# Complex products summed on GpSimd before every second inverse transform step of a long convolution

## The chip, the cores and the metric

The kernel runs on one core of one Trainium2 chip. The metric is the device time of one execution in microseconds. The engines of a core run side by side, each with an instruction queue of its own, and wait for one another through semaphores: TensorE (PE, matmuls, with its weight loads as PEld), VectorE (DVE), ScalarE (ACT), GpSimd (POOL), and SyncE (SP), which issues most of the transfers here.

## The reference

One block of a network with two halves. The first is a gated long convolution (H3), the second an MLP with a matrix over positions (gMLP). Both are modulated by vectors from a condition `c`.

```python
x = A_q                                             # 1 x 2048 x 640, bf16
sa, ca, ga, sb, cb, gb = six rows of silu(c) @ w_mod
h = layernorm(x) * (1 + ca) + sa
# first half
kv  = (causal convolution of A_k with 4 taps) * A_v
y_f = rfft(kv padded to 4096) * rfft(ssm_k padded to 4096)   # per channel, complex
y   = irfft(y_f)[:2048] + kv * ssm_D
x   = x + ga * (h * y)
# second half
h = layernorm(x) * (1 + cb) + sb
z = gelu(h @ w_in)                                  # 640 -> 2 x 864
g = w_sp @ layernorm(z[:, 864:]) + b_sp             # 2048 x 2048 over the positions
x = x + gb * ((z[:, :864] * g) @ w_out)
```

## The kernel before

The transforms are matmuls with tables of cosines and sines that the kernel makes itself. The 640 channels are worked on as five units of 128 (`u`), each in eight steps (`st`) of two frequency blocks (`KP = 2`). For a unit there is a first stage (`s1`) for the kernel's spectrum (K) and one for the signal (U), then the forward steps, the product of the two spectra, and the inverse steps. The results of the eight inverse steps are collected in `Z`; `Z` is transposed by a DMA (PE for the last unit), and a last small matmul (`y` or `yl`) gives `y`, which is multiplied into the modulated input `gh`.

```python
def forward(name, X1, st, extra=()):
    ...
        for k in range(KP):
            kc = st * KP + k
            mm(pu[:, k], M2[:, 0, kc, :], x[:, 2 * kc:2 * kc + 2, :], True, False)      # 256 columns
            mm(pu[:, k, 0], M2[:, 2, kc, :], x[:, 2 * kc + 1, :], False, False)         # 128 columns
            mm(pu[:, k, 1], M2[:, 1, kc, :], x[:, 2 * kc, :], False, True)

def u_item(u, st):
    forward(pu, "X1U%d" % u, st)

    def product(e):                       # real/imaginary of the signal x real/imaginary of the kernel
        T_ = new(T, "T", [P, KP, 2, 2, DU])                                  # bf16
        e.tensor_tensor(T_[:], tl[pu][:, :, :, None, :].to_broadcast([P, KP, 2, 2, DU]),
                        tl[KH][:, :, None, :, :].to_broadcast([P, KP, 2, 2, DU]), op=ALU.mult)
    op("D", "prod", product, r=[pu, KH], w=[T], new=[(T, "T")])

    def inv(e):
        ...
        for k in range(KP):
            kc = st * KP + k
            mm(p_[:, k], G2[:, 0, kc, :], T_[:, k, 0], True, False)          # 256 columns
            mm(p_[:, k], G2[:, 1, kc, :], T_[:, k, 1], False, False)         # 256 columns
            mm(p_[:, k, 1], G2[:, 2, kc, :], T_[:, k, 0, 0], False, False)   # 128 columns each
            mm(p_[:, k, 0], G2[:, 1, kc, :], T_[:, k, 0, 1], False, False)
            mm(p_[:, k, 1], G2[:, 0, kc, :], T_[:, k, 1, 0], False, False)
            mm(p_[:, k, 0], G2[:, 3, kc, :], T_[:, k, 1, 1], False, True)
    op("P", "inv", inv, ...)
    op("AD", "zc", ...)                   # copy of the result from PSUM into Z
```

All four partial products of a complex product are kept, and the matmuls of the inverse step add them up in PSUM.

Other operations that share the time with these:

```python
op("P", "taps", ...); op("D", "tv", ...)           # the short convolution as four matmuls, times v
op("SA", "kvw", ...)                               # kv goes to DRAM and is read back in another order
op("A", "khc", ...)                                # kernel spectrum: PSUM -> KH
op("AD", "s1c", ...)                               # first stage: PSUM -> X1
op("GD", "ghm", ...)                               # modulation of gh: a multiplication and an addition
op("D", "ym", ...)                                 # gh *= y
op("GD", "res", ...); op("D", "ln2", ...)          # residual addition, statistics of the second layernorm
op("P", "zz", ...); op("A", "gelu", ...)           # second half: z products, gelu
op("P", "fill", ...)                               # matmuls into an unused bank; they only keep PE active
```

An operation is registered with the engines on which it may run (`"GD"`: GpSimd or VectorE), what it reads and what it writes. A long list fixes which engine takes which operation and in what order; every engine works through its part of the list strictly in that order.

```python
FILLS = (4, 4, 4, 1, 2, 1, 1, 1, 3, 1, 2, 2, )
SLOTS = dict(X=4, X1=4, KH=9, T=4, Z=3, ZT=1, wm=1, big=2, dg=2, st1=2, s1=1, sm=2, pu=2, pz=2)   # buffers per kind
ORDER = """
D13 D95 D12 D96 S14 D97 D103 D109 D104 D110 A0 D115 A5 A4 A1 A2 A3 A111 D98 A99 D6 D18 P979 P980 P981 P19 S16 A112 P21
... 991 entries: a letter for the engine (P, A, D, G, S) and the number of the operation ...
"""
```

Once all of this has been issued, the mixing over the positions begins (`mix`, `project`): 32 groups of 16 matmuls of 432 columns and 32 of 7 matmuls of 320 columns, with nothing else large beside them.

Of the kernel before, what the change touches and what calls it, by code (L numbers as in the profile page):

```python
# [15 lines left out]
P = 128  # L16
# [9 lines left out]
DU = 128  # L26
# [7 lines left out]
FILLS = (4, 4, 4, 1, 2, 1, 1, 1, 3, 1, 2, 2, )  # L34
SLOTS = dict(X=4, X1=4, KH=9, T=4, Z=3, ZT=1, wm=1, big=2, dg=2, st1=2, s1=1, sm=2, pu=2, pz=2)
# [4 lines left out]
D13 D95 D12 D96 S14 D97 D103 D109 D104 D110 A0 D115 A5 A4 A1 A2 A3 A111 D98 A99 D6 D18 P979 P980 P981 P19 S16 A112 P21  # L40
D7 D8 D9 S77 D81 S78 A10 D11 G124 G125 D20 P139 A106 D82 D141 P142 A105 A140 A144 P982 P145 A146 D22 G31 D143 D116
D121 A100 G101 A118 S15 P983 P25 S17 D26 P148 S467 P23 D24 S27 A117 G107 A150 P127 D128 A149 A147 S29 G102 P984 P151
A152 P153 A154 S28 G113 S30 G119 P133 A120 G108 P157 A158 P985 P163 S79 A164 P165 A166 D471 D472 P130 D134 P155 A156
G114 P159 A131 D473 D474 P36 G43 D135 P161 D37 A160 P38 D39 P986 P167 D168 A162 A169 G129 P170 A172 P34 A171 S80 P176
A177 D178 P173 D175 P32 A174 S83 P179 D35 P187 P136 D85 P211 D180 D33 G132 P181 S468 D188 D182 A212 P191 P215 P189
A216 D192 S41 A190 P203 D204 P217 A218 P193 A194 D137 P195 S40 D196 P207 S42 P213 D208 D138 P46 P183 D184 P50 A475
P199 S84 A476 D477 D47 A214 P205 A206 P197 D200 A198 P235 A236 P221 D478 A222 D51 P44 P239 A240 P219 A220 D479 G480
P209 A210 P237 S470 D486 P223 P231 A238 A232 D45 P48 A224 D487 P241 A242 D49 S509 P510 A511 P512 A513 D488 D481 A493
S86 D88 D497 P243 D244 A498 G67 D494 P229 A230 P275 G55 A276 P201 D202 P225 A226 P185 S469 S52 D482 P263 P279 A280
P245 A186 A246 D264 D495 S514 P251 D252 P267 S87 P277 A278 D499 D268 P265 A266 P255 A122 D256 P281 A282 D500 P515 P247  # L50
D248 A483 D496 P517 D516 D537 P289 A290 D518 P299 A300 A489 P253 D254 S53 S54 P269 G616 D484 D485 G556 D490 G491 P301
A302 P62 P233 A234 D123 P227 D63 D492 A270 A228 P60 P303 P283 A304 P295 A284 D501 D502 D61 A296 P249 G558 P305 A505
S519 P293 D506 P287 A288 D507 A294 P56 A250 D57 S65 D503 P58 D59 D504 P297 A306 S89 P291 D91 P520 D535 A298 G539 P307
A292 D308 D521 G540 P339 A340 A508 G541 G536 P271 P522 D523 P257 D272 G599 P319 D320 P341 A342 P309 A310 D258 P315
D316 P343 A344 P335 D336 P68 P345 S66 D69 P273 A274 G538 D542 P259 G557 D260 P321 S64 P285 A346 D322 D562 S543 P544
D545 G563 P72 D73 A286 G595 P261 A262 P546 P347 A348 D547 P331 D332 D620 S90 P363 A364 P548 D560 P337 A338 P317 A318
G559 D549 P367 P550 D551 G554 A368 P359 A360 P327 D328 D552 G597 P70 P369 P361 A362 G655 G656 P311 P329 A330 P323 D370
D312 D324 P74 D75 D71 P351 A352 D651 S697 P365 A366 P325 A326 P357 A358 S92 D94 P333 A334 S564 D561 P565 D566 G618
G598 P371 D372 S76 S93 P403 A404 P349 A350 P567 D568 G657 D596 P313 P355 P569 A356 G619 P387 D570 G593 A314 P407 G553
A408 D388 P379 D380 P571 D572 P373 A374 P405 A406 P375 D376 P381 G578 D581 P409 A410 P391 A382 P353 D392 A354 D579  # L60
P389 G573 D576 P427 A428 P395 S601 G653 D654 A390 P377 A378 D396 P429 D600 P399 D400 P397 P383 D384 G594 S698 P602
D603 G583 A430 P431 S524 A432 P423 A424 D587 P401 A402 P415 A416 P433 A434 G588 G617 P604 D577 D575 D398 D605 P425
A426 P411 A412 D652 P393 D574 A394 P435 D436 P419 A420 P606 D607 P385 G658 P451 D452 P443 D444 D582 P608 P437 D438
A386 P417 A418 P525 P421 A422 P447 G614 G615 A526 S622 P453 A454 D609 D613 D448 P455 D456 P445 A446 P463 D464 P449
P459 P457 D460 D580 G611 G621 A450 P413 D610 A414 P623 D624 P439 D440 A458 P465 P625 D626 P461 D462 A466 P441 S527
A442 P627 D628 P528 A529 P665 D666 S530 P663 D664 P629 D630 P659 P661 D662 D631 D632 D633 A660 P987 P667 D668 P676
G555 D669 P683 D670 D671 D699 P690 D700 D672 D684 P531 A532 P533 D634 G701 D702 D703 D704 P705 D673 A534 D706 D674
D715 P988 P713 A714 P711 D712 P989 P709 A710 G636 D675 D635 P707 D708 P990 P763 A764 P731 A732 D716 D677 D640 D637
P759 G717 D718 D691 D720 D719 D678 P729 A730 P723 A724 D681 A760 P741 A742 P765 D682 D784 D679 P725 A726 D639 D641
P727 A728 P761 D781 D680 A766 G646 P721 A722 D638 D783 D782 D586 D648 G785 D786 D787 A788 D789 A762 P738 D790 A739  # L70
S791 P734 P767 A768 D685 D686 P773 A774 A735 P745 A746 D688 P752 A753 P755 A756 D687 D736 A792 D743 P748 G612 A794
D642 A749 D740 D744 P769 D584 D643 D847 P771 A772 D793 D795 D796 P825 A826 A770 D585 P839 A840 P797 A798 D644 P837
A838 P807 P814 A808 D692 P827 A828 A815 P833 A834 D689 P829 A830 D696 D849 D757 D592 D645 P835 A836 D848 D850 G851
D695 D852 D853 D855 D856 D854 D809 S857 P804 A805 D694 D733 D590 D914 D589 D647 P800 A801 D754 P831 A832 D693 D913
D650 A858 D816 D859 D860 D861 P811 A812 P821 A822 P818 D862 P866 P887 D649 A819 P863 A888 A864 D916 D591 D915 G917
P870 D806 A871 D918 D919 D920 D922 D921 A867 P877 D813 D817 D868 P899 D758 D872 A900 P905 A878 A906 D747 S923 D925
D924 D750 P880 A881 A927 D928 P873 A874 D875 P901 D802 A902 P903 A904 D810 D926 P884 A885 P929 A930 P946 D820 D823
A947 P932 A933 D876 P893 A894 D882 P939 P950 D751 A940 P959 P957 D737 G775 A951 A958 D879 D883 A960 D799 P897 A898
D934 P943 A944 D803 D824 D776 D889 D777 D886 G841 D842 P953 A845 P936 A937 A954 A780 P963 A964 D948 D846 P895 A896
A843 D778 P969 D890 P971 A972 D865 D869 G907 D908 D911 D909 D910 A970 P891 A892 A779 P967 P965 A966 D912 D955 D952  # L80
D956 D938 D945 D949 D941 D942 D931 D935 G973 A844 D974 A977 D976 D975 A126 P961 A962 A968 D978
# [39 lines left out]
def kernel(  # L121
# [80 lines left out]
    with ExitStack() as actx:  # L202
# [56 lines left out]
        mbase = consta.tile([P, KCH, QH], F32, name="mbase")  # L259
# [4 lines left out]
        nc.gpsimd.iota(pint[:], [[0, 1]], base=0, channel_multiplier=1)  # L264
        nc.gpsimd.iota(f1k[:], [[4, NKC], [0, 2]], base=1, channel_multiplier=0, allow_small_or_imprecise_dtypes=True)
        nc.gpsimd.iota(f1r[:], [[0, NKC], [16, 2]], base=48, channel_multiplier=0, allow_small_or_imprecise_dtypes=True)
        nc.gpsimd.memset(mpi[:], -2.0 * HALF_PI)
        nc.gpsimd.iota(pidx[:], [[0, 1]], base=0, channel_multiplier=1, allow_small_or_imprecise_dtypes=True)
        nc.gpsimd.iota(fidx[:], [[1, P]], base=0, channel_multiplier=0, allow_small_or_imprecise_dtypes=True)
        nc.gpsimd.iota(mbase[:], [[4, KCH], [64, QH]], base=1, channel_multiplier=0, allow_small_or_imprecise_dtypes=True)  # L270
# [44 lines left out]
        def m2_base():  # L315
            def steps(e):
                e.tensor_scalar(mstep[:, 0:NCH], fidx[:, 0:NCH], pidx[:, 0:1], 4.0 * KCH / 8192.0, op0=ALU.mult, op1=ALU.mult)
                e.tensor_scalar(mstep[:, NCH:], mstep[:, 0:NCH], 0.25, None, op0=ALU.add)
                e.tensor_scalar(mturn[:], mstep[:], TWO_PI, None, op0=ALU.mult)
            op("D", "mstep", steps, w=["mstep"])  # L320
            op("D", "mbase", lambda e: e.tensor_scalar(mbase[:], mbase[:], pidx[:, 0:1], 1.0 / 8192.0, op0=ALU.mult, op1=ALU.mult),
               w=["mbase"])

        def m2_chunk(i):
# [4 lines left out]
            def turns(e):  # L329
                new(a, "T", [P, 2, KCH, QH], F32)  # L330
                for h in range(2):
                    e.tensor_scalar(tl[a][:, h], mbase[:], mstep[:, h * NCH + i:h * NCH + i + 1], MAGIC, op0=ALU.add, op1=ALU.add)
            op("DG", "turns", turns, r=["mbase", "mstep"], w=[a], new=[(a, "T")])
            op("D", "msub", lambda e: e.scalar_tensor_tensor(tl[a][:], tl[a][:], MAGIC, mbase[:, None].to_broadcast([P, 2, KCH, QH]),
# [104 lines left out]
        def u_item(u, st):  # L439
# [4 lines left out]

            def product(e):
                T_ = new(T, "T", [P, KP, 2, 2, DU])
                e.tensor_tensor(T_[:], tl[pu][:, :, :, None, :].to_broadcast([P, KP, 2, 2, DU]),  # L447
                                tl[KH][:, :, None, :, :].to_broadcast([P, KP, 2, 2, DU]), op=ALU.mult)
            op("D", "prod", product, r=[pu, KH], w=[T], new=[(T, "T")])

            def inv(e):
# [4 lines left out]
                for k in range(KP):  # L456
                    kc = st * KP + k
                    mm(p_[:, k], G2[:, 0, kc, :], T_[:, k, 0], True, False)
# [527 lines left out]
```

## Time and profile before

| | |
|---|---|
| time, median of three runs | 336.73 us (336.67 to 336.78) |
| span of the profiled execution | 335.4 us |
| PE busy | 320.8 us, 96% |
| DVE busy | 222.7 us, 66% |
| ACT busy | 140.2 us, 42% |
| POOL busy | 72.7 us, 22% |
| mean granted clock of PE | 0.995 |

The profile is of one execution. Busy times are shares of the whole span, and the span has stages that look quite different: convolution, z products, mixing. So the views by stretch of time say more than these totals. Matmuls are pipelined, and a matmul that waits inside PE counts as busy. In a row of a group of instructions stand the line of the kernel, the engine, the operation, output and input, how many, the time busy and the mean in ns; after the last bar stands how long the engine was idle just before these instructions, and what ended that. In the table by stretch each row has the stretch, its length, then busy time and (x) instructions of PE, PEld, DVE, ACT and POOL, the granted clock of PE, the DMA share and GB/s.

### The profile page before, as it was taken

What the parts mean: (1) busy time and instruction counts of PE and PEld (TensorE: products, weight loads), DVE (VectorE), ACT (ScalarE), POOL (GpSimd) and SP (SyncE); (2) the same over time, 40 slices, a digit from 0 to 9 for tenths busy, and PEclk for the clock granted to TensorE, in tenths of its full rate; (3) what the DMA queues carried; (4) which work ended last, traced back from release to release, by engine and by line L of the source; (5) the groups of instructions that cost most, each with busy time, mean ns of one, the idle gap of its engine ahead of it and who ended that gap; (6) DMA issues with size and microseconds to landing.
All of it is one profiled execution on the core that took longest, in us unless ns stands there. A gap on an engine that the chain in (4) does not pass through costs nothing.

```text
span 335.4 us, 6584 instructions
## 1 busy us (share of the span) xinstructions
PE 320.8 (96%) x2712; PEld 214.3 (64%) x2719; DVE 222.7 (66%) x468; ACT 140.2 (42%) x242; POOL 72.7 (22%) x89
## 2 busy tenths in 40 slices
PE   6799999999989999999999999999999999999995
PEld 1467879878879899845555555555555555555553
DVE  7987999899999999997885775263222332223323
ACT  2774999975657754257765669000000000000000
POOL 2560040447694903222101121000000000000000
PEclk9999999999999999989999999999999999999999
DMA  8999998999767836302145900995555657532221
GB/s 143 183 201 228 217 309 202 251 215 242 173 143 157 264 64 163 102 2 48 32 78 79 191 0 3 215 220 132 118 117 121 133 131 131 110 49 47 49 47 59
DMA packets 128581, 45.00 MB, mean 134 GB/s; under 512 B 117704, under 2 KB 127784, under 8 KB 128552
## 3 DMA queue, kind: packets, MB, share of 16 engines
q1 hardware_dynamic: 126592, 44.59, 61.5%
q8 instruction: 21, 0.34, 0.4%
q10 hardware_dynamic: 1960, 0.01, 0.3%
q14 instruction: 8, 0.07, 0.1%
HBM read 16.11 MB, written 5.24 MB: 64 GB/s over the span
## 4 chain that ended last, share of the span: by engine, by line
PE 73%; DVE 17%; DMA 5%; issue 2%; POOL 1%; ACT 0%; DVEq 0%; SPq 0%; ACTq 0%
PE ps L918 28%; PE pz L237 15%; PE pu L237 14%; PE po L936 9%; DVE T L447 5%; PE sm L237 4%; PE s L237 2%; DVE big L517 2%; DMA D_col<-in_A_ssm_D_dram 2%; DMA big<-in_A_k_dram 1%; DMA X<-kv_scr 1%; DVE X L240 1%; DVE gh L623 1%; DVE st L666 1%; DMA kv_scr<-big 1%
## 5 line engine op out<-in xcount | busy, mean ns | idle before, releaser
L918 PE MATMUL ps<-X,wT 128*128 128x432 bf16 x512 | 95.7, 346 | 0.0
L918 PEld LDWEIGHTS <-wT 128*128 128x128 bf16 x512 | 50.0, 98 | 42.2
L929 ACT COPY uT<-pt 128x896 bf16<-128x896 bf16 x1 | 0.9, 905 | 116.9 <-PE pt L928 116.9
L237 PEld LDWEIGHTS <-Z 128*128 128x128 bf16 x320 | 31.1, 98 | 27.7 <-issue 1.1
L447 DVE TENSOR_TENSOR T<-pu,KH 128x1024 bf16<-128x1024 f32 x40 | 47.7, 1217 | 1.4 <-PE pu L237 1.0
L237 PE MATMUL pu<-X,M 128*128 128x128 bf16 (+1 forms) x480 | 45.5, 237 | 0.8 <-DVE T L447 0.7
L237 PE MATMUL pz<-T,G 128*128 128x128 bf16 (+1 forms) x480 | 41.2, 237 | 0.7 <-DVE T L447 0.6
L237 PEld LDWEIGHTS <-M 128*128 128x128 bf16 x480 | 37.1, 98 | 6.2 <-issue 1.3
L921 DVE SCALAR_TENSOR_TENSOR u<-ps,bcol,G 128x432 bf16<-128x432 f32 x18 | 12.0, 668 | 42.2 <-PE ps L918 42.2
L237 PEld LDWEIGHTS <-G 128*128 128x128 bf16 x480 | 35.3, 98 | 3.6 <-DVE T L447 0.8
L240 ACT CAST X<-s 128x1024 bf16<-128x1024 f32 x31 | 31.5, 1015 | 11.2 <-PE s L237 11.0
L936 PE MATMUL po<-w_o,uT 128*128 128x320 bf16 (+1 forms) x224 | 32.8, 299 | 0.0
L237 PE MATMUL pz<-big,Z 128*128 128x432 bf16 x160 | 32.3, 346 | 0.5 <-ACT M L856 0.5
L237 PE MATMUL pu<-big,Z 128*128 128x432 bf16 x160 | 32.6, 347 | 0.0
L921 DVE SCALAR_TENSOR_TENSOR u<-ps,bcol,M 128x432 bf16<-128x432 f32 x14 | 9.3, 667 | 29.5 <-PE ps L918 29.5
L936 PEld LDWEIGHTS <-uT 128*128 128x128 bf16 (+1 forms) x224 | 21.8, 98 | 9.8
L240 ACT CAST KH<-pu 128x512 bf16<-128x512 f32 x40 | 22.9, 596 | 10.1 <-PE pu L237 10.0
L938 DVE TENSOR_TENSOR ot<-po,xt 128x320 bf16<-128x320 f32 x32 | 15.7, 491 | 13.4 <-PE po L936 13.4
L240 ACT CAST Z<-pz 128x512 bf16<-128x512 f32 x32 | 18.6, 590 | 10.4 <-PE pz L237 10.0
L862 DVE BATCH_NORM_STATS2 stz<-X 128x6 f32<-128x432 bf16 x32 | 18.2, 586 | 6.8 <-ACT X L856 6.8
L237 PE MATMUL sm<-big,dg 128*128 128x512 bf16 (+3 forms) x73 | 20.0, 380 | 1.3 <-DVE big L517 0.5
L623 POOL TENSOR_TENSOR gh<-gh,gca_bf 128x512 bf16<-128x512 bf16 x14 | 16.8, 1202 | 16.9 <-DVE gca_bf L610 12.9
(141 smaller groups left out, 380.6 us busy)
## 6 DMA issues: line engine op xcount, KB each, us to landing
wm<-in_w_mod_dram SPq DMA_DIRECT2D x6, 800.0 KB, 5.8
xt<-in_A_q_dram SPq DMA_DIRECT2D x4, 640.0 KB, 6.3
out_dram<-ot SPq DMA_DIRECT2D x16, 160.0 KB, 2.3
big<-in_B_w_in_dram SPq DMA_DIRECT2D x2, 1080.0 KB, 6.9
X<-in_A_ssm_k_dram SPq DMA_DIRECT2D x4, 512.0 KB, 8.7
kv_scr<-big SPq DMA_DIRECT2D x4, 512.0 KB, 3.4
X<-kv_scr SPq DMA_DIRECT2D x4, 512.0 KB, 5.2
w_o<-in_B_w_out_dram SPq DMA_DIRECT2D x6, 160.0 KB, 3.0
```

Source lines behind the costliest of these rows:

```text
L237: nc.tensor.matmul(o, lhsT=w, rhs=x, start=start, stop=stop)
L240: (e.copy if e is nc.scalar else e.tensor_copy)(dst, src)
L447: e.tensor_tensor(T_[:], tl[pu][:, :, :, None, :].to_broadcast([P, KP, 2, 2, DU]), tl[KH][:, :, None, :, :].to_broadcast([P, KP, 2, 2, DU] ...
L517: e.tensor_tensor(vsl, tl[ps][:], vsl, op=ALU.mult)
L623: lambda e, vec=vec, o=o: e.tensor_tensor(gvu, gvu, vec[:, None, d0:d0 + du].to_broadcast([P, TB, du]), op=o),
L666: op("D", "ln2", lambda e, n=n: e.bn_stats(out=st2[:, n, (0, 0, 0, 1, 2)[u], :], in_=xt[:, n, us[0] * DU:(u + 1) * DU]), r=[("xt", (v, n)) ...
L862: op("D", "stz", lambda e, i=i, n=n, fc=fc: e.bn_stats(out=stz[:, n, fc, :], in_=tl[z2][:, i, fc * FC:(fc + 1) * FC]), r=[(z2, (i, fc))], ...
L918: nc.tensor.matmul(ps[:, :FC], lhsT=wTs[t][:, s_, :], rhs=tl["z2_%d" % (s_ // TB)][:, s_ % TB, fc * FC:(fc + 1) * FC], start=(s_ == 0), st ...
L921: nc.vector.scalar_tensor_tensor(u[:, sl], ps[:, :FC], bcol[:, t:t + 1], z1[t][:, sl], op0=ALU.add, op1=ALU.mult)
L929: nc.scalar.copy(uTs[t][:], pt[:])
L936: nc.tensor.matmul(ps[:, :HS], lhsT=uTs[t][:fsz[ft], ft, :], rhs=w_o[:fsz[ft], ft, h * HS:(h + 1) * HS], start=(ft == 0), stop=(ft == NFT ...
L938: nc.vector.tensor_tensor(ot[:, h * HS:(h + 1) * HS], ps[:, :HS], xt[:, t, h * HS:(h + 1) * HS], op=ALU.add)
```

## The change

In steps 1, 3, 5 and 7 of every unit (20 of the 40), the product is written in float32 to a buffer of its own (`Tf`). Two further operations then make the real part (a difference) and the imaginary part (a sum) of the complex product out of the four partial ones, in float32, and write them in bf16 to `W`. They may run on GpSimd or VectorE. The inverse step then has three matmuls per frequency block rather than six, since PSUM no longer needs to add the partial products up. The aim is to take matmul work off PE; only half the steps get it, to keep the other engines from filling up.

Around it:

- `X` and `T` have three buffers rather than four, which makes room for `Tf` and `W`.
- A table for the transform's angles (`mbase`) moves to a `KH` buffer, and is made by an operation of the list; the small tables `pidx` and `fidx` are made ahead of larger ones on GpSimd.
- The transposed results of the last unit lie in `X` buffers, two to a buffer, rather than in `T`.
- The whole list is new (1031 entries). Among other things the loads at the start come in another order. It was chosen by how it does when operations are delayed at random.
- There are 11 fillers with 30 matmuls in all, rather than 12 with 26.

```diff
-FILLS = (4, 4, 4, 1, 2, 1, 1, 1, 3, 1, 2, 2, )
-SLOTS = dict(X=4, X1=4, KH=9, T=4, Z=3, ...)
+FILLS = (4, 4, 4, 1, 2, 4, 2, 1, 4, 2, 2, )
+SUMS = (1, 3, 5, 7)
+SLOTS = dict(Tf=2, W=2, X=3, X1=4, KH=9, T=3, Z=3, ...)
 ORDER = """
 (all of it replaced)
@@ start @@
-        mbase = consta.tile([P, KCH, QH], F32, name="mbase")
         nc.gpsimd.iota(pint[:], ...)
+        nc.gpsimd.iota(pidx[:], ...)
+        nc.gpsimd.iota(fidx[:], ...)
         nc.gpsimd.iota(f1k[:], ...)
         nc.gpsimd.iota(f1r[:], ...)
         nc.gpsimd.memset(mpi[:], -2.0 * HALF_PI)
-        nc.gpsimd.iota(pidx[:], ...)
-        nc.gpsimd.iota(fidx[:], ...)
-        nc.gpsimd.iota(mbase[:], ...)
+            op("G", "mbi", base, w=["mbase"], new=[("mbase", "KH")])
@@ u_item @@
+            summed = st in SUMS
+            ttag = "Tf" if summed else "T"
             def product(e):
-                T_ = new(T, "T", [P, KP, 2, 2, DU])
+                T_ = new(T, ttag, [P, KP, 2, 2, DU], F32 if summed else BF16)
                 e.tensor_tensor(... op=ALU.mult)
+            if summed:
+                def total(e, o):
+                    if o == 0:
+                        new(W, "W", [P, KP, 2, DU])
+                    T_ = tl[T]
+                    e.tensor_tensor(tl[W][:, :, o, :], T_[:, :, 0, o, :], T_[:, :, 1, 1 - o, :],
+                                    op=ALU.add if o else ALU.subtract)
+                op("GD", "csum", lambda e: total(e, 0), r=[T], w=[(W, 0), (W, "new")], new=[(W, "W")])
+                op("GD", "csum", lambda e: total(e, 1), r=[T, (W, "new")], w=[(W, 1)])
             def inv(e):
                 for k in range(KP):
                     kc = st * KP + k
+                    if summed:
+                        w_ = tl[W]
+                        mm(p_[:, k], G2[:, 0, kc, :], w_[:, k], True, False)
+                        mm(p_[:, k, 1], G2[:, 2, kc, :], w_[:, k, 0], False, False)
+                        mm(p_[:, k, 0], G2[:, 1, kc, :], w_[:, k, 1], False, True)
+                        continue
                     mm(p_[:, k], G2[:, 0, kc, :], T_[:, k, 0], True, False)
                     (five more as before)
@@ last_stage_pe @@
                 def keep(e, pt=pt, ZT=ZT, low=low):
-                    new(ZT, "T", [P, QB, P])
-                    copy(e, tl[ZT][:], tl[pt][:])
+                    if low:
+                        new(ZT, "X", [P, 2 * QB, P])
+                    copy(e, tl[ZT][:, (0 if low else QB):(QB if low else 2 * QB), :], tl[pt][:])
```

## The prediction

> **What bounds the kernel now.** I read the slices of the page first, to see the stages.
>
> ```profile
> PE   6799999999989999999999999999999999999995
> PEld 1467879878879899845555555555555555555553
> DVE  7987999899999999997885775263222332223323
> ACT  2774999975657754257765669000000000000000
> POOL 2560040447694903222101121000000000000000
> ```
>
> A slice is 8.4 us. Up to about slice 18 (150 us) PE and DVE are both at 9. After that PE alone is full: first the z products of the MLP, then the mixing. So only the first 150 us can gain from a change in the convolution, and there two engines compete for the title of bound. The chain of waits gives the fixed part:
>
> ```profile
> 206.86 17.52 PE ps L918 x96
> ```
>
> Mixing starts at 206.86 of 335.4 us, with PE without a gap from there: 128.5 us which this change does not touch. The timeline shows where the z products start (columns: start, busy):
>
> ```profile
> 145.88 3.19 PE L237 MATMUL pu<-big,Z 128*128 128x432 bf16 x15
> ```
>
> From 145.88 to 206.86 are 61.0 us. The 64 z groups of five matmuls take 64 x 0.912 = 58.4 us (0.912 from a steady stretch of the chain, "0.91 PE pz L237 x5"), so only 2.6 us there are waits and transposes. The time is thus **the start of the z products plus about 189 us**. What sets that start? The busy time by stretch:
>
> ```profile
> 30.00:40.00 10.00, 9.89 (x113) 8.34 (x112) 9.95 (x13) 7.26 (x14) 0.00 (x0) 1.00 1.08 194
> 50.00:60.00 10.00, 10.00 (x122) 9.08 (x120) 9.63 (x14) 9.21 (x15) 0.00 (x0) 1.00 0.90 215
> 90.00:100.00 10.00, 8.86 (x100) 7.15 (x100) 9.86 (x11) 4.77 (x8) 9.92 (x9) 1.00 0.73 160
> 120.00:130.00 10.00, 10.00 (x161) 9.53 (x157) 9.80 (x12) 4.06 (x8) 3.62 (x3) 1.00 0.70 142
> ```
>
> The third number is PE's busy time, the seventh DVE's. Between 30 and 150 us DVE adds up to 115.7 of 120 us. PE looks as full, but its busy time counts waiting matmuls. By columns at the rate seen (twelve matmuls of 2048 columns in 0.88 us), the work of PE ahead of the first z product is 40 inverse steps x 0.88, 80 forward x 0.44, 40 first-stage x 0.44, 20 taps x 0.86, and some 20 us of small things and fillers: about 125 us of 146. For DVE I weighted every entry ahead of the first z product in the operation list with the mean of its row: 145.8 us. Records of neighbours overlap by some hundredths (two products take 2.35 us, not 2.43), so the true need is about 140. **DVE is the bound of the convolution**, PE second with some 20 us of slack, though in the last third (115 to 134 us) the chain runs through PE: pairs of inverse and forward steps.
>
> The rows that matter for the change, kept apart by shape and by engine:
>
> ```profile
> L447 DVE TENSOR_TENSOR T<-pu,KH 128x1024 bf16<-128x1024 f32 x40 | 47.7, 1217 | 1.4 <-PE pu L237 1.0 <-issue 0.2
> L237 PE MATMUL pz<-T,G 128*128 128x128 bf16 x320 | 30.9, 220 | 0.0
> L237 PE MATMUL pz<-T,G 128*128 128x256 bf16 x160 | 30.6, 273 | 0.7 <-DVE T L447 0.6
> L623 POOL TENSOR_TENSOR gh<-gh,gca_bf x14: 1151/1158/1419, 62.1 to 115.5; 128x512 bf16<-128x512 bf16 x14
> L623 DVE TENSOR_TENSOR gh<-gh,gca_bf x6: 407/420/1359, 61.2 to 97.0; 128x512 bf16<-128x512 bf16 x6
> L623 DVE TENSOR_TENSOR gh<-gh,gsa_bf x6: 410/764/1358, 80.9 to 118.4; 128x512 bf16<-128x512 bf16 x6
> ```
>
> The last two (min/median/max ns) show a price that means hide: the same DVE operation takes 0.41 us alone and up to 1.36 us.
>
> **What the Trainium skill says.** "SBUF — State Buffer", section "Who interferes with whom": a DVE instruction with two SBUF inputs, or in a two-port mode, and a GpSimd instruction that reads SBUF exclude each other for a whole instruction; with one SBUF input DVE isn't hit. The trace agrees: the product (one input from PSUM) keeps 1206 to 1226 ns, while the row above goes to 1359, which is 0.41 plus most of one 1.16 us GpSimd operation. "GPSIMD Engine Reference", section "Elementwise — side-by-side cycle accounting": a two-input tensor_tensor costs about 2.6 cycles an element, 4497 ns for 2048 float32. Here GpSimd takes 1.16 us for 512 bf16, or 2.26 ns an element with its overhead, against 2.2 there. "TensorE: Matmul & The Clock Gate", section "Wait — 56ns, not 53.3ns?": a warm matmul occupies columns / 2.4 GHz + 2.5 ns. For an inverse step: 2048 / 2.4 + 12 x 2.5 = 883 ns, and the trace has 0.88.
>
> **The change, part by part.**
>
> *PE.* In 20 of 40 inverse steps two wide and four narrow matmuls per frequency block become one wide and two narrow: 12 matmuls of 2048 columns become 6 of 1024, or 0.44 us. 20 x 0.44 = **8.8 us less**. Fillers go from 26 to 30 matmuls of 512 columns: +0.9 us. PE ahead of the z products: 125.4 to 117.7 us. As PE wasn't the bound, most of this becomes slack; it is worth time only where PE ended the wait, as near 60 to 70 us (1.5 us of idle DVE) and 115 to 134 us.
>
> *The products.* Same 1024 elements from PSUM, written as float32 rather than bf16. One element a cycle either way (1217 ns for 1024): **0**.
>
> *The sums.* 40 of 256 elements. Reading the new list entry by entry: 37 stand on GpSimd, 3 on DVE. GpSimd small operations take 0.19 us (L182) and 512 elements 1.16, so 256 come to about 0.68 us, an estimate: 37 x 0.68 = 25 us. Together with what moves away (five modulations, two residual additions and so on, -9.6, and +1.4 others) GpSimd goes from 60 to 77 us ahead of the z products. It has room, unless the order of its queue delays a sum. A pair then lies 1.4 us between product and inverse step; the list puts other forward and inverse steps between, so I count nothing for it.
>
> *DVE, the sum that decides.* By the same weighting, entries ahead of the first z product: three sums +1.2; five more modulations +2.1; evacuations of first-stage and inverse results moved to ACT -2.6 and -2.7; one ln1 statistic to ACT -1.2; one diagonal -0.7; one transposed copy to ACT -0.7; tables and sign flips +1.0; final multiplications earlier +1.3, ln2 statistics later -1.4; rest about -0.2. Sum: 145.8 to 142.0, **-3.8 us**. At the last product the list stands at 128.2 against 131.5, so it is gained before the tail.
>
> *ACT.* 104 to 113 us of 146: idle enough.
>
> *Contention.* Modulations on DVE go from 12 to 17, and GpSimd is busy about 63% of the middle rather than 52%. The 12 took 8.7 us where 12 x 0.42 is 5.0, an excess of 0.31 each. At somewhat more each, the excess grows from 3.7 to 5.3: **+1.6 us**, some of it also on other two-input operations.
>
> *Start.* ident waited 1.0 us for fidx; the new order puts that iota earlier and the large one later: -0.5 us. The first forward operand comes through DRAM (kv_scr) after four loads; these come partly after the kernel spectra now. DVE idled 2.6 us between 20 and 30; the new list fills with table work, but the loads may land later. I count 0 beside the 0.5.
>
> *PE's relief and the tail.* Some 0.5 us from waits on PE, and 0.5 us because the table load for gelu (1.28 us at 146.1, after the first z product) comes ahead of it.
>
> Sum: -3.8 + 1.6 - 0.5 - 1.0 = **-3.7 us**. Since a list is never followed perfectly I take a little off: **-3.4, 333.3 us** (ratio 0.990).
>
> **Rivals.**
>
> *PE was the bound.* Then all of 8.8 - 0.9 = 7.9 us show: 329 us. For it: PE at 9.9 or 10 in most stretches, and the chain through PE from 115 to 134. Against: DVE at 9.6 to 9.9 in the same stretches, and its list time of 145.8 beside an actual start at 145.88. To pass PE's gain on, DVE would have to lose 8 us as well.
>
> *GpSimd takes the place.* Sums queue behind 1.16 us modulations in one in-order queue; only two float32 buffers, so a late sum stops the second next product on DVE, and three buffers for X and T rather than four. If each of 20 steps cost DVE 0.3 us: +6, or 339 us. For it: at 90 to 100 us GpSimd was already busy 9.92 of 10. Against: most forward and inverse steps in the list are placed around the sums, and the order is said to be chosen under random delays.
>
> *The start slips.* With the first loads reordered a late transposed load or DRAM round trip moves everything by 1 to 3 us: 334 to 336 us. The first 30 us show a DMA share of 77 to 110%, so an order that loads the spectra first can delay kv.
>
> *The PE clock drops.* PE with 8 us less work could be throttled in gaps, as it was at 140 to 145 us (0.66 of full). The tail there has few matmuls in both lists and fillers in both: up to 2 us either way.
>
> **Range and chances.** Centre 333.3. Half of PE's gain on top gives 330; GpSimd waits or a slipped start together with no gain give 337. So 329.5 to 337.5 for 8 in 10. Faster by over 2% needs 330.0 or less: 0.12. Slower by over 2% needs over 343.5: 0.04. Within: 0.84.
>
> **What would show it.** The z products should start at 142 to 143.5 us rather than 145.88, and mixing run the same 128.5 us. Products at 1.21 to 1.23 us in both types; summed inverse steps at 0.44 us; GpSimd sums at 0.6 to 0.75 us; DVE still above 95% between 30 and 140 us and PE visibly below what it was (under 9.5). Modulations on DVE with a mean well over 0.42 us. Wrong: DVE idle for sums or float32 buffers, PE idle on GpSimd for over 3 us in all, a first product later than 30.2 us by over 1 us, or DVE staying as long as before.

## The result, and the profile after

The changed kernel took 334.72 us (median of four runs, 334.26 to 334.89) beside 336.75 us for the kernel before on the same chip: **ratio 0.9937, 95% interval 0.992 to 0.9955**. The prediction had 333.3 us in a range of 329.5 to 337.5. The gain is there, 2.0 us instead of 3.4, but its parts are quite different from those predicted, as the milestones of the two profiles show. The bracketed numbers are the lengths of the stages between them, as differences of the rounded milestones.

| us | first product | last product | first z product | first mixing matmul | span |
|---|---|---|---|---|---|
| before | 30.2 | 131.5 (101.3) | 145.9 (14.4) | 206.7 (60.8) | 335.4 (128.7) |
| after | 32.6 | 124.5 (91.9) | 142.3 (17.8) | 203.8 (61.5) | 332.8 (129.0) |
| difference | +2.4 | -9.4 | +3.4 | +0.7 | +0.3 |

So the stretch with the 40 products, which the change is about, became 9.4 us shorter, and a later start, a longer tail and a few tenths at the end gave 6.8 us of it back. Both numbers were far from the prediction's; their difference was near it, and that was luck.

The slices of the page after (8.3 us each), with the granted clock:

```profile
PE   6699999999999998699999899999999999999995
...
DVE  6579999999999998989876783262223222233323
...
POOL 2251733659489695551111111000000000000000
PEclk9699999999999999999999999999999999999999
```

The second slice has a granted clock of 6, which the prediction did not reckon with: something happened to PE at the start. GpSimd now works from the fourth slice on. After slice 18 PE stands as full as before. The chain of waits has the mixing, and the timeline the first z product (start, length):

```profile
203.92 17.52 PE ps L945 x96
```

```profile
142.27 1.08 PE L240 MATMUL pz<-big,Z 128*128 128x432 bf16 x5
```

Both stages after the convolution kept their length to within 0.7 and 0.3 us. The stretches that were shown of before:

```profile
30.00:40.00 10.00, 9.52 (x97) 7.56 (x96) 9.75 (x13) 8.45 (x18) 4.55 (x6) 1.00 1.14 266
50.00:60.00 10.00, 10.00 (x123) 8.96 (x121) 9.44 (x17) 9.97 (x18) 3.42 (x5) 1.00 0.97 234
90.00:100.00 10.00, 10.00 (x123) 8.42 (x122) 9.96 (x16) 6.91 (x11) 8.44 (x9) 1.00 0.69 188
...
120.00:130.00 10.00, 9.13 (x131) 7.84 (x130) 9.08 (x12) 5.65 (x11) 9.64 (x10) 1.00 1.04 268
```

PE lost 8.8 us of matmuls and still shows 9.1 to 10 (a matmul that waits counts as busy, and the same work now stands in a shorter stretch). The rows of the products, the sums and the summed inverse steps:

```profile
L465 POOL TENSOR_TENSOR W<-Tf 128x256 bf16<-128x256 f32 x37 | 27.4, 760 | 27.7 <-DVE Tf L456 26.1 <-PE pz L240 1.6
...
L456 DVE TENSOR_TENSOR T<-pu,KH 128x1024 bf16<-128x1024 f32 x20 | 24.2, 1213 | 0.5 <-PE pu L240 0.5
L456 DVE TENSOR_TENSOR Tf<-pu,KH 128x1024 f32<-128x1024 f32 x20 | 24.0, 1215 | 0.9 <-PE pu L240 0.8
...
L240 PE MATMUL pz<-W,G 128*128 128x128 bf16 x80 | 9.9, 219 | 0.0
L240 PE MATMUL pz<-W,G 128*128 128x256 bf16 x40 | 9.9, 273 | 0.4 <-DVE W L465 0.4
```

A product costs 1.21 us in either type. A sum takes 0.76 us on GpSimd, and the last bar of the last row says that PE waited 0.4 us in all for sums, and for one of the three on DVE at that. The few sums and the modulations that run on DVE (min/median/max ns), from the two lines' own views:

```profile
L465 DVE TENSOR_TENSOR W<-Tf x3: 572/1370/1454, 83.5 to 126.2; 128x256 bf16<-128x256 f32 x3
```

```profile
L648 DVE TENSOR_TENSOR gh<-gh,gca_bf x10: 407/412/1208, 68.5 to 108.9; 128x512 bf16<-128x512 bf16 x10
L648 DVE TENSOR_TENSOR gh<-gh,gsa_bf x7: 409/426/951, 71.0 to 110.3; 128x512 bf16<-128x512 bf16 x7
```

17 modulations took 9.0 us on DVE (10 x 0.544 + 7 x 0.514, their means), 1.9 over 17 x 0.42. Before, 12 of them had an excess of 3.7. GpSimd disturbs the modulations less, though it is busier there; the norms that make `gh` went a little the other way (mean 0.50 us, 0.44 before).

### The profile page after: what moved, and what is told of

Read it like the earlier page. It is cut to its first block, busy times and chain, and to the rows that moved or that the text cites. A ratio compares the mean times of both kernels' runs of the same rounds, so it can differ in the third digit from the quotient of the medians.

```text
span 332.8 us, 6423 instructions
## 1 busy us (share of the span) xinstructions
PE 314.2 (94%) x2596; PEld 206.7 (62%) x2603; DVE 218.8 (66%) x466; ACT 147.0 (44%) x257; POOL 93.5 (28%) x120
## 4 chain that ended last, share of the span: by engine, by line
PE 74%; DVE 14%; DMA 6%; issue 2%; ACT 2%; ACTq 0%; DVEq 0%
PE ps L945 28%; PE pu L240 15%; PE pz L240 12%; PE po L963 9%; PE sm L240 6%; DMA Z<-Z 4%; DVE Tf L456 3%; PE s L240 3%; DVE T L456 2%; DMA D_col<-in_A_ssm_D_dram 2%; DMA big<-in_A_k_dram 1%; DVE gh L648 1%; DVE W L465 1%; DVE st L569 1%; DVE big L542 1%
## 5 line engine op out<-in xcount | busy, mean ns | idle before, releaser
L956 ACT COPY uT<-pt 128x896 bf16<-128x896 bf16 x1 | 0.9, 905 | 117.5 <-PE pt L955 117.5
L240 PE MATMUL pu<-X,M 128*128 128x128 bf16 (+1 forms) x480 | 46.2, 237 | 1.7 <-DVE Tf L456 1.1
L465 POOL TENSOR_TENSOR W<-Tf 128x256 bf16<-128x256 f32 x37 | 27.4, 760 | 27.7 <-DVE Tf L456 26.1
L243 ACT CAST X<-s 128x1024 bf16<-128x1024 f32 x32 | 32.8, 1024 | 4.5 <-PE s L240 4.4
L948 DVE SCALAR_TENSOR_TENSOR u<-ps,bcol,M 128x432 bf16<-128x432 f32 x14 | 9.3, 667 | 30.9 <-PE ps L945 30.9
L240 PEld LDWEIGHTS <-G 128*128 128x128 bf16 x360 | 26.8, 98 | 2.2 <-DVE W L465 0.5
L456 DVE TENSOR_TENSOR Tf<-pu,KH 128x1024 f32<-128x1024 f32 x20 | 24.0, 1215 | 0.9 <-PE pu L240 0.8
L965 DVE TENSOR_TENSOR ot<-po,xt 128x320 bf16<-128x320 f32 x32 | 15.7, 492 | 13.4 <-PE po L963 13.4
L456 DVE TENSOR_TENSOR T<-pu,KH 128x1024 bf16<-128x1024 f32 x20 | 24.2, 1213 | 0.5 <-PE pu L240 0.5
L243 ACT CAST Z<-pz 128x512 bf16<-128x512 f32 x36 | 20.8, 592 | 6.3 <-PE pz L240 6.1
L240 PEld LDWEIGHTS <-X 128*128 128x128 bf16 x288 | 18.2, 99 | 8.3 <-DVE X L395 4.0
L240 PE MATMUL sm<-big,dg 128*128 128x512 bf16 (+3 forms) x73 | 21.4, 407 | 0.6 <-DVE big L542 0.2
```

The lines of the kernel that those rows point to most:

```text
L240: nc.tensor.matmul(o, lhsT=w, rhs=x, start=start, stop=stop)
L243: (e.copy if e is nc.scalar else e.tensor_copy)(dst, src)
L465: e.tensor_tensor(tl[W][:, :, o, :], T_[:, :, 0, o, :], T_[:, :, 1, 1 - o, :], op=ALU.add if o else ALU.subtract)
L948: nc.vector.scalar_tensor_tensor(u[:, sl], ps[:, :FC], bcol[:, t:t + 1], z1[t][:, sl], op0=ALU.add, op1=ALU.mult)
L956: nc.scalar.copy(uTs[t][:], pt[:])
L965: nc.vector.tensor_tensor(ot[:, h * HS:(h + 1) * HS], ps[:, :HS], xt[:, t, h * HS:(h + 1) * HS], op=ALU.add)
```

## The experiments

Two theories stood against each other at first. A: the new list brings the gain, by taking work from DVE, and PE's relief is slack. B: the arithmetic brings it, by taking work from PE. What is given below beside a ratio is its 95% interval. The lengths of stages are from one profile of each variant:

| us | first product | product stretch | tail to first z product | span |
|---|---|---|---|---|
| e1_list_alone | 32.2 | 100.9 | 18.4 | 342.7 |
| e2_sums_left_out | 31.8 | 94.4 | 17.5 | 333.9 |
| e3_sums_on_dve | 31.8 | 111.2 | 17.2 | 350.4 |
| e7_sums_in_old_list | 29.5 | 112.4 | 17.6 | 349.1 |
| e8_old_pe_relief | 30.5 | 99.9 | 13.6 | 333.6 |
| e9_old_dve_relief | 29.6 | 98.5 | 14.0 | 331.7 |
| e10_old_both_reliefs | 30.0 | 98.4 | 13.5 | 331.5 |
| e4_start | 30.9 | 91.8 | 17.8 | 331.0 |
| e5_quiet_tail | 31.6 | 91.9 | 16.2 | 329.0 |
| e6_start_and_tail | 29.1 | 91.9 | 16.3 | 326.3 |
| e11_all_sums_gpsimd | 29.3 | 91.2 | 15.7 | 325.2 |

**The new list without the new arithmetic** (`e1_list_alone`).

```diff
-SLOTS = dict(Tf=2, W=2, ...)
+SLOTS = dict(Tf=5, ...)
-                T_ = new(T, ttag, [P, KP, 2, 2, DU], F32 if summed else BF16)
+                T_ = new(T, ttag, [P, KP, 2, 2, DU], BF16)
 def total(e, o):                                    # both sums
-    e.tensor_tensor(tl[W][:, :, o, :], ...)
+    pass
 inv:
-                    if summed:                      # three matmuls
+                    if False:                       # six matmuls of T_ in every step
```

> The changed kernel with its new list, but the old arithmetic: no sums, all products in bf16, six matmuls per frequency block in every inverse step (five bf16 buffers stand in for Tf and W). PE has 8.8 us more to do than in the changed kernel, GpSimd 27 us less, DVE the same less two or three sums. Theory A (DVE bounds the convolution, PE's saving is nearly all slack): the first z product comes 0 to 2 us later than at 142.3, the time is 334 to 337 us, so the new list alone holds most of the 2.0 us. Theory B (PE is the bound and its saving is what was gained): 8 to 9 us later, 342 to 344 us.

Measured: 342.85 us, ratio 1.0177 [1.0153, 1.0202]. The list by itself is slower than the kernel before, and its product stretch of 100.9 us is the old 101.3. The product stretches of the kernel before, of the changed kernel and of this variant, in this order:

```profile
30.19:131.54 101.35, 98.37 (x1216) 85.52 (x1219) 97.34 (x154) 73.24 (x117) 47.59 (x42) 1.00 0.89 205
32.62:124.47 91.85, 89.52 (x1101) 77.01 (x1108) 89.96 (x148) 75.32 (x124) 60.93 (x68) 1.00 0.94 214
32.21:133.07 100.86, 98.58 (x1213) 85.70 (x1214) 93.09 (x148) 76.12 (x123) 37.90 (x35) 0.98 0.86 194
```

DVE, the seventh number, is busy for 97.3 us before, 90.0 us with the change and 93.1 us here. So the list does take work from DVE, but where PE keeps its old work, DVE stands idle for 7.8 us of the stretch, most of it waiting for PE (4.0 us before, 1.9 with the change). PE's matmuls in the stretch come to 95 us before, 95 us here and 85 us with the change. That is an estimate: the columns of all matmul records there, at the 0.88 us for 2048 columns that an inverse step takes (a few records may be missing). PE's own work alone thus keeps this stretch from becoming much shorter. A falls, B holds.

The profile is of the slowest of five runs (344.8 us), and in it the granted clock of PE was 0.5 from 114.9 to 118.3 us. An inverse step then took 1.91 us instead of 0.88:

```profile
113.01 0.60 PE L240 MATMUL pu<-X,M 128*128 128x256 bf16 x6 [1.13 <-DVE T L456]
114.14 0.60 PE L240 MATMUL pu<-X,M 128*128 128x256 bf16 x6 [0.53 <-DVE Tf L456]
...
115.16 1.91 PE L240 MATMUL pz<-T,G 128*128 128x256 bf16 x12
```

The clock is not what makes this variant slow: its one run with the mean clock of the changed kernel, 0.99, took 342.23 us.

**The sums left out** (`e2_sums_left_out`). The summed steps keep three matmuls, which read the first pair of bf16 products in place of the sums. Half of the complex product is thus left out of these steps.

```diff
-SLOTS = dict(Tf=2, W=2, ...)
+SLOTS = dict(Tf=5, ...)
-                T_ = new(T, ttag, [P, KP, 2, 2, DU], F32 if summed else BF16)
+                T_ = new(T, ttag, [P, KP, 2, 2, DU], BF16)
 def total(e, o):
-    e.tensor_tensor(tl[W][:, :, o, :], ...)
+    pass
 inv:
-                        w_ = tl[W]
+                        w_ = tl[T][:, :, 0]
```

> The changed kernel with three matmuls per summed step, but the sums left out: the inverse step reads the first pair of products in bf16, so part of the computation is missing. It has PE's saving without GpSimd's 27 us. Theory A (the sums cost only what they block on DVE, by sharing SBUF access): 1 to 2 us faster than the changed kernel, 333 to 334 us, with modulations and norms on DVE nearer to 0.42 us. Rival C (the inverse steps wait for the sums in GpSimd's queue): 4 us faster or more, 330 us. Rival D (the sums cost nothing): 334.4 to 335.0 us.

Measured: 335.92 us, ratio 0.9963 [0.9946, 0.9981]. The change with all its sums has 0.9937 [0.992, 0.9955]: the 27.4 us of GpSimd work cost nothing on the path. Theory D comes nearest, though the time is 0.9 us above its range. Against the variant before it only matmuls are gone (8.8 us of them), and the time fell by **6.9 us** (342.85 to 335.92). That is what PE's relief is worth in this list. That the stretch is longer without sums (94.4 against 91.9 us) was not expected. The buffers and the places of the GpSimd operations in time differ too, and in this profile the clock of PE was halved for 3.4 us within the stretch:

```profile
110.20:113.60 3.40, 3.40 (x26) 2.78 (x25) 3.40 (x5) 1.76 (x3) 3.24 (x3) 0.50 1.03 364
```

No run separates these.

**All sums on DVE** (`e3_sums_on_dve`). The 37 sums that GpSimd makes go to DVE, at the same places of the list.

```diff
-G<csum> x37, D<csum> x3
+D<csum> x40
```

> All 40 sums on DVE at the same places of the list; else the changed kernel. DVE gets 37 operations of 256 float32 elements, some 0.35 us each by size, 13 us in all. Theory A (DVE bounds the convolution): 10 to 14 us slower, 345 to 349 us, and PE visibly idle. Theory B (PE bounds, DVE has room): under 339 us.

Measured: 351.92 us, ratio 1.0436 [1.0416, 1.0457]. That is above even Theory A's 349. The product stretch grew by 19.3 us (111.2 against 91.9), and DVE was busy for 107.2 us of it rather than 90.0. So DVE has no room in this list either: with the change, both PE and DVE hold the stretch.

**The arithmetic in the old list** (`e7_sums_in_old_list`). The operations of the changed kernel (the small changes to tables and transposes too) in the order of the kernel before, with the two sums put on GpSimd right behind each product of a summed step, and the old fillers. Buffers: `X=4, T=4, W=3`, products in bf16.

```diff
 old list, at each product of steps 1, 3, 5, 7:
 D<prod>
+G<csum> G<csum>
 inv: three matmuls of W, as in the change
```

> The arithmetic alone: the list of the kernel before, with the two sums of every summed step put on GpSimd right behind its product and three matmuls in the inverse step (products in bf16, since four X and four T buffers leave no room for float32 ones; three W buffers). PE has 8.8 us less to do, DVE the same. Theory A (PE and DVE bound the convolution together, each in its turn, so relief of one alone gives little, and the old list has inverse steps too close behind their products for two sums of 0.7 us): first product to last product 100 to 104 us rather than 101.3, time 336 to 341 us. Theory B (PE's saving is what gained, as the run with the list alone was 8 us slower than the change): that stretch 93 to 97 us, time 330 to 333 us.

Measured: 350.62 us, ratio 1.0414 [1.0398, 1.0431], worse than any theory had it. Who waited between 30 and 160 us (us in total, times, longest):

```profile
PE pz L239 <- POOL W L464: 7.4, 6, 3.1
...
DVE st L690 <- POOL xt L684: 5.1, 3, 2.5
PE pz L239 <- DVE T L455: 4.9, 2, 4.6
...
DVE gh L664 <- POOL gh L647: 3.6, 2, 2.6
```

The inverse step stands close behind its product in the old list, made for an inverse step that needs nothing between them. Now PE, whose queue is in order, stands before `W` for up to 3.1 us, and everything behind it waits. DVE waits 8.7 us for residual additions and modulations that stand in GpSimd's queue with the sums, and the granted clock of PE was halved for 17 us in all between 113 and 158 us. The rival of the prediction in which GpSimd takes the place is real in this list; the new list avoids it with other work between product and inverse step (0.4 us of waiting in all).

**What held the old list?** PE's relief (`e8_old_pe_relief`), DVE's relief (`e9_old_dve_relief`), and both (`e10_old_both_reliefs`), in the kernel before with its own list. The first leaves out three of six matmuls in every second inverse step (8.8 us of PE); the second leaves out the 12 modulations that stood on DVE (8.7 us).

```diff
 inv, PE's relief:
+                    if st % 2:
+                        mm(p_[:, k], G2[:, 0, kc, :], T_[:, k, 0], True, False)
+                        mm(p_[:, k, 1], G2[:, 2, kc, :], T_[:, k, 0, 0], False, False)
+                        mm(p_[:, k, 0], G2[:, 1, kc, :], T_[:, k, 0, 1], False, True)
+                        continue
 gh_mod, DVE's relief:
-   lambda e, vec=vec, o=o: e.tensor_tensor(gvu, gvu, ...)
+   lambda e, vec=vec, o=o: e is nc.gpsimd and e.tensor_tensor(gvu, gvu, ...)
```

> The kernel before with its own list, and one thing less: in every second inverse step three of the six matmuls of a frequency block are left out (those that read the second half of the products), 8.8 us of TensorE work in all; nothing is added. Theory P, that of the prediction (VectorE was the bound, TensorE had slack): 336 to 337 us, the product stretch 100.8 to 101.3. Theory R (TensorE was the bound): 328 to 330 us, the stretch 93 to 94. Theory C (both engines hold each other, in different places): 334 to 336 us, the stretch 98.5 to 100.5, with VectorE busier in it than before.

> The kernel before with its own list, and one thing less: the 12 modulations that stood on VectorE are left out (8.7 us of its busy time); those on GpSimd stay. Theory P (VectorE was the bound): 328 to 330 us, the product stretch 93 to 94.5. Theory R (TensorE was the bound): 336 to 337 us. Theory C (both hold each other): 333 to 336 us, the stretch 98 to 100.5.

> The kernel before with its own list and both things left out: three of six matmuls in every second inverse step, and the 12 modulations on VectorE. Theory P: as with the modulations left out alone, within 0.7 us. Theory R: as with the matmuls left out alone, within 0.7 us. Theory C: clearly more than the sum of the two gains, 327 to 331 us, the product stretch 92 to 95.

Measured, beside 336.8 us: PE's relief 335.42 us, 0.9956 [0.9943, 0.9968]; DVE's 333.84 us, 0.991 [0.9898, 0.9923]; both 331.47 us, 0.9846 [0.9826, 0.9866]. Gains of 1.4, 3.0 and 5.3 us. P and R both fall for the old list: neither engine hands on more than about a third of what is taken from it. C had the single ones right, but was too hopeful for both (the stretch 98.4 us where it said 92 to 95; that profile is of the longest of its five runs). Nor can 5.3 be told from 1.4 and 3.0 together, as each interval reaches 0.4 to 0.7 us to either side. The product stretches with PE's relief, with DVE's and with both:

```profile
30.49:130.40 99.91, 93.03 (x1114) 78.31 (x1112) 96.92 (x154) 72.95 (x117) 47.58 (x42) 1.00 0.91 208
29.56:128.06 98.50, 97.86 (x1221) 85.46 (x1219) 90.03 (x142) 73.14 (x117) 46.52 (x42) 1.00 0.92 211
29.99:128.37 98.38, 92.61 (x1115) 78.40 (x1112) 90.60 (x142) 72.84 (x117) 46.50 (x42) 1.00 0.97 211
```

With PE relieved, DVE stays as busy as before (96.9 us). With DVE relieved, PE is busy for 97.9 of 98.5 us. Each stands right behind the other. With 17.5 us of work gone from both, PE is idle for 5.8 us and DVE for 7.8, and most of the stretch stays: the old order seems to hold the two engines to one another, which is argued and not shown. Between 30 and 129 us DVE now waits with both left out:

```profile
DVE gh L645 <- PE sm L237: 2.1, 4, 0.8
DVE T L447 <- ACT KH L240: 1.6, 1, 1.6
DVE T L447 <- PE pu L237: 1.5, 6, 0.5
DVE nmr L569 <- POOL rstd L183: 1.3, 1, 1.3
```

Four small waits for three different engines, no single bound. So PE's relief was worth 1.4 us in the old list and 6.9 us in the new; the new list alone 0.4 us of the stretch (101.3 to 100.9), and on top of PE's relief 5.5 us (99.9 to 94.4). List and arithmetic gain only together.

**The start** (`e4_start`). In the changed kernel the timeline of PE, and the waits for the entire execution, show where the 2.4 us arise:

```profile
11.06 0.59 PE L240 MATMUL pz<-F1bd,X 128*128 128x256 bf16 x2 [3.99 <-DVE F1bd L295]
...
12.29 3.62 PE L240 MATMUL sm<-big,dg 128*128 128x512 bf16 x8
...
17.58 1.90 PE L240 MATMUL sm<-big,dg 128*128 128x512 bf16 x8
```

```profile
DVE X L395 <- DMA D_col<-in_A_ssm_D_dram: 2.8, 1, 2.8
```

The first operation of DVE that needs the small transfer of `D_col` (the factors `ssm_D`) stood there until 10.06 us; the mask `F1bd` is behind it in DVE's queue, and PE's first useful matmul behind that. PE was idle for 3.99 us. After that eight matmuls of the taps took 3.62 us, where the next eight take 1.90. The granted clock is the third number from the end:

```profile
7.10:10.00 2.90, 0.00 (x0) 0.00 (x0) 0.19 (x1) 2.83 (x11) 0.19 (x1) 1.00 1.25 131
10.00:11.00 1.00, 0.00 (x0) 0.11 (x1) 0.94 (x3) 0.00 (x0) 0.87 (x2) 0.52 1.28 287
11.00:16.80 5.80, 5.74 (x19) 2.71 (x19) 3.99 (x10) 2.42 (x6) 1.18 (x2) 0.50 0.79 210
```

The Trainium skill, "TensorE: Matmul & The Clock Gate", Part 1, says that PE falls to half its clock after an idle window of some 3.4 us. The halving agrees. But the clock fell here when PE had been idle for 3 us, and with the list alone (above) after waits of 1.1 and 0.5 us, so by these profiles a wait need not last 3.4 us to cost the clock. The variant puts work that needs no `D_col` ahead:

```diff
 list, at the start (P PE, D DVE, A ACT):
-A<diag u0> ... P<first stage of u0> ... P<taps u0> P<taps u0>
+D<diag u0> right behind the cast of the tap values
+P<taps u0> P<taps u0> ahead of P<first stage of u0>
-D<add D, u0> ... A<angles, F1> D<mask, F1> ... D<turns> D<msub>
+A<angles, F1> D<mask, F1> D<turns> D<msub> ahead of D<add D, u0>
```

> The changed kernel with the start mended: the first two short-convolution taps ahead of the first first-stage group on PE, the first diagonal on DVE straight after its coefficients rather than on ACT, and the small table for the first stage ahead of the operation that waits for D_col. In the changed kernel the first product starts at 32.6 us against 30.2 before, and PE's clock is halved at 10 to 16 us. Theory A (DVE-bound chain from the first product on, so a late start moves everything): first product 1.5 to 3 us earlier, no dip of the clock, time 332 to 333.5 us. Rival E (the late start is made up later because DVE's work is only reordered): 334.3 to 335 us.

Measured: 331.79 us, ratio 0.985 [0.9834, 0.9866], that is 2.9 us better than the change and a little better than Theory A had it. The mean clock of its four runs is 0.993 to 1.000, where the changed kernel's were 0.989 to 0.990. The first product came at 30.9 us, and the taps (timeline of this variant) run at full speed from 7.48 us:

```profile
7.48 1.90 PE L239 MATMUL sm<-big,dg 128*128 128x512 bf16 x8 [1.27 <-DVE dg L526]
```

**The tail** (`e5_quiet_tail`). In the changed kernel, DVE from 125 us on, and GpSimd in the same time:

```profile
125.72 1.86 DVE L465 TENSOR_TENSOR W<-Tf 128x256 bf16<-128x256 f32 x2
...
136.44 1.11 DVE L800 SCALAR_TENSOR_TENSOR nmr<-mv,rstd 128x2 f32<-128x2 f32 x1
137.48 1.35 DVE L812 TENSOR_SCALAR Z<-xt,mv,rstd 128x640 bf16<-128x640 bf16 x1
138.75 1.24 DVE L685 TENSOR_TENSOR xt<-xt,gh 128x256 bf16<-128x256 bf16 x1
...
148.76 3.26 DVE L812 TENSOR_SCALAR Z<-xt,mv,rstd 128x640 bf16<-128x640 bf16 x4
```

```profile
136.38 3.45 POOL L685 TENSOR_TENSOR xt<-xt,gh 128x512 bf16<-128x512 bf16 x3
...
147.66 3.46 POOL L685 TENSOR_TENSOR xt<-xt,gh 128x512 bf16<-128x512 bf16 x3
```

Three residual additions of 1.15 us each stand on GpSimd exactly where DVE has the short operations that the first z products need. Each DVE operation waits out one of them: one on two numbers a partition takes 1.11 us. The variant moves GpSimd's additions away and gives GpSimd the two last sums:

```diff
 list (G GpSimd, D DVE):
-D<csum u4 st1> x2
+G<csum u4 st1> x2
-G<resid u3> G<resid u2> behind the first rstd of the second norm
+G<resid u3> G<resid u2> ahead of it
-G<resid> x4 in the tail
+D<resid> x4
```

> The changed kernel with another division between GpSimd and DVE after the last product. There, six residual additions of GpSimd (1.15 us each) run under DVE operations of two SBUF inputs or of a two-port form: nmr takes 1.04 to 1.11 us rather than 0.14, one norm 1.35 rather than 0.43, four norms 3.26 rather than 1.5. Here two of the additions move ahead of the first rstd on GpSimd, four go to DVE, and the two sums of the last step go from DVE (1.86 us) to GpSimd. Theory A (that blocking is what makes the tail 3.4 us longer than before): last product to first z product 14 to 16 us rather than 17.8, norms all near 0.43 us, the z products without the wait for the first transposed load, 330.5 to 333 us. Rival F (the tail is bound by its dependencies, not by the blocking): 334.3 to 335.5 us.

Measured: 329.96 us, ratio 0.9808 [0.9785, 0.9831], or 4.8 us better than the change by the medians (4.3 by the ratios), though DVE has four more additions (and two sums less). The same DVE operations in this variant:

```profile
135.74 0.16 DVE L799 SCALAR_TENSOR_TENSOR nmr<-mv,rstd 128x2 f32<-128x2 f32 x1
135.82 0.44 DVE L811 TENSOR_SCALAR Z<-xt,mv,rstd 128x640 bf16<-128x640 bf16 x1
136.18 0.28 DVE L684 TENSOR_TENSOR xt<-xt,gh 128x256 bf16<-128x256 bf16 x1
...
145.72 1.52 DVE L811 TENSOR_SCALAR Z<-xt,mv,rstd 128x640 bf16<-128x640 bf16 x4
```

1.11, 1.35 and 1.24 us became 0.16, 0.44 and 0.28. The tail shortened by 1.6 us (17.8 to 16.2), and the z stage by 1.3 (61.5 to 60.2) since the norms for its later groups come in time. Another 1.0 us of this profile is the first product at 31.6 rather than 32.6 us with an unchanged start: it spreads by that much between executions. The variant moves the additions and the last sums at once. Without any sums (`e2_sums_left_out`) the tail was still 17.5 us, which speaks for the additions. 1.8 us of the tail, against 14.4 before, stay unexplained. The last sums may be part of it, as nothing is left to hide them: the last inverse step ends 3.4 us after the start of the last product here, and 2.4 us before the change.

**Both repairs** (`e6_start_and_tail`).

```diff
-list of the change
+list of the change with both sets of moves
```

> The mended start and the mended tail together. If the two gains are independent, as they lie in different stages: the gain of the start (2.9 us by ratio) and that of the tail add up, 328 to 330.5 us. If the earlier start only shifts which transfers collide later: 331 to 332 us.

Measured: **328.04 us, ratio 0.9735 [0.9722, 0.9748]**. The gains add up within their intervals (2.9 and 4.3 us by the ratios, 6.8 together), and this version beats both kernels.

**The last sum on DVE** (unit 2, step 5; `e11_all_sums_gpsimd`) also goes to GpSimd.

```diff
-D<csum u2 st5>
+G<csum u2 st5>
```

> The variant with the start and the tail mended (328.0 us), and the last sum that still stood on VectorE (1.45 us there, 0.37 of it work) given to GpSimd. If a sum on VectorE costs its whole duration: 326.8 to 327.3 us. If GpSimd's own queue is what holds that place: 328 to 329 us.

Measured: 327.88 us, ratio 0.9749 [0.9714, 0.9784]. No difference from the version above can be seen in this interval. The single profile is 1.1 us shorter, which settles nothing.

## Why the prediction was right, point by point

- **What bounds the convolution: wrong as put.** The prediction had one bound, DVE, with PE some 20 us slack. PE's sum of 125 us was right, but its slack does not lie where the products are. Estimated as above, PE has 20 us of matmuls in the 30.2 us ahead of the first product, 95 in the 101.3 us of the stretch and 9 in the tail of 14.4, so 6 us of the slack are in the stretch. In the old list neither relief passed on more than 3.0 us; in the new list PE's relief is worth 6.9 us, and 37 sums more on DVE cost 17 us (334.72 to 351.92). Two engines are full, and the order decides how much of a relief is handed on. The comparison "list time of 145.8 beside an actual start at 145.88" looked like proof. But with overlapping records counted once, DVE was busy for 135.2 us of that time.
- **PE's relief: the term that was mis-sized.** 8.8 us less and 0.44 us a step were right. "Most of this becomes slack", with 0.5 us counted, was wrong for the new list by over 6 us.
- **DVE's list sum, -3.8 us: right in size, but not passed on by itself.** DVE's busy time ahead of the first z product fell from 135.2 to 130.8 us. In the product stretch it fell from 97.3 to 90.0 us, and rose from 13.2 to 16.8 in the tail. The list alone took 0.4 us off the product stretch, as DVE then waited for PE. Together with PE's relief the stretch lost 9.4 us, more than either term, and what is left of it is DVE's busy time and 1.9 us.
- **Products, 0: right** (1.21 us in both types). **Sums hidden: right**; 0.76 us each instead of 0.68, and no gain was seen from leaving them out.
- **Contention, +1.6 us: right size of thing, wrong place.** On the modulations it fell from 3.7 to 1.9 us. It came back in the tail, where residual additions on GpSimd stretch the operations that the first z products need: the tail grew by 3.4 us, of which moving those operations and two sums took back 1.6, with 1.3 more in the z stage. The cause named, the exclusion of two engines in "SBUF — State Buffer", "Who interferes with whom", was right, and the trace shows it on a norm (0.43 to 1.35 us) and on a tiny operation too (that one took 1.08 us before the change as well). That it would gather where GpSimd's last operations meet DVE's shortest chain was not looked for.
- **Start, -0.5 us: wrong sign.** It was +2.4 us in the profiles. The rival "the start slips" had its size (1 to 3 us) but another cause than was named: a small transfer at the head of DVE's queue and the clock of PE after it, rather than kv's way through DRAM. "A first product later than 30.2 us by over 1 us" was listed as a sign of error, and it came.
- **Fixed stages: right.** z products started at 142.3 us (142 to 143.5 was said), mixing took 129.0 us. The table load for gelu did come ahead (132.94 rather than 146.12 us), but its -0.5 us was covered by late norms: the z stage is 61.5 us with the change, 60.2 with the quiet tail, 60.8 before.
- **PE under 9.5: wrong** in three of four stretches, as a shorter stretch fills it again.

So the sum was near because errors cancelled: -9.4 us instead of -3.8 + 1.6 - 0.5 (PE) in the stretch, and +2.4, +3.4 and +1.0 at the start, in the tail and after it, where -1.0 was counted. Two figures of the prediction are slightly off: DVE's busy time from 30 to 150 us is 114.8 us and not 115.7, and 125.4 us less 7.9 is 117.5 and not 117.7. Nothing rests on either.

## What to carry to other kernels

When two engines are both over 90% busy in a stage, do not name one of them the bound from its busy time alone: leave work out of each by turns, in the same order, and see what comes back. Count an engine's slack in the stage that the change is in: of PE's 20 us only some 6 lay there. The worth of a relief belongs to the order, so new arithmetic needs a new order and has to be judged with it. In a list chosen by machine, look at the first matmul and at the last short chain by themselves, since 6.7 us lay there, which the middle did not show. Keep long GpSimd operations away from the short DVE chain that the next stage waits for.

## What the runs showed of the hardware

- A DVE operation of 128 x 2 elements with two SBUF inputs takes 0.14 to 0.16 us alone and 1.11 us beside one 1.15 us GpSimd operation: what is lost does not shrink with the operation.
- The granted clock of PE was halved when PE had been idle for 3 us, and in another run after waits of 1.13 and 0.53 us. Eight matmuls of 512 columns then took 3.62 instead of 1.90 us, an inverse step 1.91 instead of 0.88; waiting for a small transfer thus cost twice.
- GpSimd needs 0.73 us for the sum of 256 float32 pairs, and 0.67 us for bf16 pairs (`e7_sums_in_old_list`; medians both): the type makes 8% there.
